# 48 unused matmuls of several tile shapes behind the last output matmul of an attention-plus-SwiGLU kernel

## The chip, the cores and the metric

The kernel runs on one core of one Trainium2 chip. A core has a matrix engine (TensorE, PE in the profile; its weight loads are listed apart as PEld), VectorE (DVE), ScalarE (ACT), GpSimd (POOL) and SyncE (SP), each with its own instruction queue, and 16 DMA engines that the queues feed. The engines meet through semaphores. The metric is the device time of one execution in microseconds, the median over several runs.

TensorE's array has 128 rows (the inputs of a matmul, the contracted dimension) and 128 columns (its outputs). A matmul can be given a part of it, a *tile*: "64x128" is a tile of 64 rows and 128 columns, and its place is named by its first row and column. The stationary operand (the weights) is loaded into the tile, and then the moving operand streams through, one column after another; the result goes to a bank of PSUM. In the profile's rows the tile stands ahead of the shape of the moving operand: `64*128 64x512`.

## The reference

One transformer block with its two branches side by side, for 2048 tokens of width 576, in bf16:

```python
x = A_x
xn = _layernorm(x, axis=-1)
return x + _A_ref(xn, A_wqkv, A_wo) + _B_ref(xn, B_w1, B_w3, B_w2)
```

Branch A is causal attention with 32 heads of 18 and a window of 256 tokens, followed by the projection `wo`; branch B is a gated unit, `silu(xn @ w1) * (xn @ w3)`, 4608 wide, followed by `w2`.

## The kernel before

The kernel writes all instructions into a list by hand, in program order (`_Prog.add`, line 59): each with its engine, the buffers that it reads (`r`), writes anew (`w`) or writes jointly with the ones before (`j`). `resolve` (line 90) works out from these the fewest semaphore waits: a `w` or `j` on a PSUM bank waits for the other engines' reads of what stood there before, while the order within TensorE's own queue needs no semaphore. `replay` (line 130) then issues each engine's list in its own block, and SyncE at its end waits for all output transfers. At the end of the block all engines meet; the instructions of this meeting carry line 1283 in the profile.

The tokens are worked in four chunks of 512. In each chunk TensorE computes the projections to q, k and v, the attention scores (line 621) and the products with v (line 689) in between the 36 units of the gated branch (line 759), and then the second half of the chunk: for both halves of the output's 576 columns, and for four token tiles of 128, it sums `hT @ w2` and `oT @ wo` in one PSUM bank a token tile (`p2_list`, `p2_mm`, line 830). The scores, the units and most of the second half use 64x128 tiles, two at a time, one in each half of the rows. The products with v use 64x20 tiles, eight at a time: two halves of the rows by four groups of columns.

The end of the last chunk is different (`whole` in `p2_list`): the four token tiles are finished one after the other with 128x128 tiles. For token tiles 0 to 2, VectorE adds the residual from the bank to the output buffer `ofin` (line 861) and SyncE sends it (line 863). The last token tile has its sum so far added to the residual ahead of time (`keep`, line 845), and its last part is computed in two cuts of 160 and 128 columns, into two other banks, `ACC[0][0]` and `ACC[0][1]`; each cut is added (line 852) and sent (line 854) by itself. So behind the very last matmul stand one addition over 128 columns, one transfer of 32 KB, SyncE's wait for it, and the meeting of the engines.

The eight PSUM banks in the second half are `ACC[0]` (four banks, first half of the columns) and `ACC[1]` (four banks, second half). `oT` holds the attention's output, transposed, 128 partitions by 5 by 512.

Of the kernel before, what the change touches and what calls it, by code (L numbers as in the profile page):

```python
# [44 lines left out]
class _Prog:  # L45
# [13 lines left out]
    def add(self, eng, fn, r=(), w=(), j=(), dma=None, after=()):  # L59
        deps = []  # L60
        for k in r:
            deps += self.bufs[k].writers
        for k in w:
            g = self.bufs.get(k)
            if g is not None:
                deps += g.ahead(eng)
        for k in j:
            g = self.bufs[k].before
            if g is not None:
                deps += g.ahead(eng)  # L70
        op = _Op(eng, fn, deps + list(after), dma)
        op.after = tuple(after)
        self.n[eng] += 1
        op.pos = self.n[eng]
        if dma is not None:
            self.dma_count[dma] = self.dma_count.get(dma, 0) + 16
            op.cnt = self.dma_count[dma]
        for k in r:
            self.bufs[k].readers.append(op)
        for k in w:  # L80
            self.bufs[k] = _Gen([op], self.bufs.get(k))
        for k in j:
            self.bufs[k].writers.append(op)
        for k in w:
            if self.bufs[k].before is not None:
                self.bufs[k].before.before = None
        self.ops.append(op)
        return op
# [76 lines left out]
def bass_parallel_sum__sliding_block__glu_gated_swiglu__prompt_kernel(  # L165
# [20 lines left out]
    G = H // 4  # L186
# [9 lines left out]
    add = P.add  # L196

    with ExitStack() as es:

        def sb(name, shape, dtype=dt.bfloat16):  # L200
            return es.enter_context(nc.sbuf_tensor(name, shape, dtype))
# [68 lines left out]
        oT = sb("oT", [128, 5, CH])  # L270
# [7 lines left out]
        PS = es.enter_context(nc.psum_tensor("ps", [128, 8, 512], dt.float32))  # L278
        JOBS, SC = ((0, 1), (2, 3), (4, 5)), (6, 7)
        ACC = [[], []]  # L280
# [36 lines left out]
        def load_part(after=(), behind=()):  # L317

            nonlocal nfill
            if nfill >= 6 * NC * NFC:  # L320
                return
            k, i = divmod(nfill, 6)
            s, dst = w13_at(k)
            part, n = divmod(i, 2)
            c0 = (k % NFC) * 512
            src = (B_w3, B_w1)[n]
            nfill += 1
            add("sp", lambda e: e.dma_start(
                dst[64 * n:64 * n + 64, 3 * part:3 * part + 3, :],
                src[192 * part:192 * part + 192, c0:c0 + 512].rearrange("(kd p) f -> p kd f", p=64)),  # L330
                r=list(behind), after=after, dma=f"w13_{s}_{n}", **{"j" if i else "w": [("w13", s)]})
# [5 lines left out]
        def last_pe():  # L337
            return next(o for o in reversed(P.ops) if o.eng == "pe")
# [546 lines left out]
        for t in range(TB):  # L885
# [4 lines left out]
            w=["wv"], dma="wv")  # L890
# [24 lines left out]
        for h in range(2):  # L915
            for n in range(2):
                c0 = n * D + h * HD
# [137 lines left out]
        for c in range(NC):  # L1055
# [13 lines left out]
            start = START[c]  # L1069
# [119 lines left out]
            for u in range(NF):  # L1189
# [46 lines left out]
                if c == 0 and u == 13:  # L1236
                    for t in range(4):
                        r0 = 4 * Dh + 252 * (t // 2)
                        rows = A_wo[r0:r0 + 252, :].rearrange("(s p d) f -> p s d f", p=2, d=Dh)[t % 2, :, :, :]
                        add("sp", lambda e, t=t, rows=rows: e.dma_start(wo[0:126, t, :], rows),  # L1240
                            dma="wo", **{"j" if t else "w": ["wo"]})
                if c == 0 and u == 18:
                    rows = A_wo[0:4 * Dh, :].rearrange("(n d) f -> n d f", d=Dh)
                    add("sp", lambda e: e.dma_start(wo[126:128, 0:4, :], rows[:, 0:2, :].rearrange("n d f -> d n f")),
                        j=["wo"], dma="wo")
                    for p in range(2):
                        add("sp", lambda e, p=p: e.dma_start(wo[64 * p:64 * p + 64, 4, :], rows[:, 2:Dh, :]),
                            j=["wo"], dma="wo")
# [12 lines left out]
            n = -3  # L1261
            for item in p2_list(c):
# [17 lines left out]
                elif n in (170, 195, 220, 245, 270, 295) and c + 1 < NC:  # L1280
                    load_part((last_pe(),))

        with nc.Block() as block:
            P.replay(es, block)

# [27 lines left out]
```

## Time and profile before

| what | value |
|---|---|
| time, median of 3 runs | 554.75 us (554.68 to 554.92) |
| span of the profiled execution, first to last instruction | 553.1 us |
| the page's own time for the profiled execution, beside the span | none given |
| TensorE busy | 549.3 us (99%) |
| mean granted TensorE clock | 1.000 |
| matmuls, weight loads | 8072, 8072 |
| chain of waits, share of TensorE | 98% |

A row of the view in order of time gives start and length in microseconds from the start of the span, engine, line, operation, the names of its output and inputs, the shapes, and the number of instructions that the row merges; in brackets the idle time ahead of it. A group row gives line, engine, operation, names, shapes and count, then busy microseconds and the mean nanoseconds of one. A matmul's length is from its start to the end of its result, so rows of matmuls that follow each other overlap: the pace is read from start to start.

### The profile page before, as it was taken

What the parts mean: (1) busy time and instruction counts of PE and PEld (TensorE: products, weight loads), DVE (VectorE), ACT (ScalarE), POOL (GpSimd) and SP (SyncE); (2) the same over time, 40 slices, a digit from 0 to 9 for tenths busy, and PEclk for the clock granted to TensorE, in tenths of its full rate; (3) what the DMA queues carried; (4) which work ended last, traced back from release to release, by engine and by line L of the source; (5) the groups of instructions that cost most, each with busy time, mean ns of one, the idle gap of its engine ahead of it and who ended that gap; (6) DMA issues with size and microseconds to landing.
All of it is one profiled execution on the core that took longest, in us unless ns stands there. A gap on an engine that the chain in (4) does not pass through costs nothing.

```text
span 553.1 us, 18357 instructions
## 1 busy us (share of the span) xinstructions
PE 549.3 (99%) x8072; PEld 338.3 (61%) x8072; DVE 313.7 (57%) x584; ACT 258.7 (47%) x360; POOL 212.2 (38%) x388
## 2 busy tenths in 40 slices
PE   8999999999999999999999999999999999999998
PEld 6555544777555544577765554558886555455776
DVE  8466797710468886651056988665105567866311
ACT  6456776000288567700047847760005784775000
POOL 6324675400047465530005656643001553663100
PEclk9999999999999999999999999999999999999999
DMA  9998899477577953757746875466773673542750
GB/s 257 211 200 175 190 222 200 129 200 181 141 144 141 181 135 96 181 144 206 185 110 139 175 144 146 117 149 168 191 180 87 138 172 103 150 105 57 194 152 23
DMA packets 128038, 86.00 MB, mean 155 GB/s; under 512 B 35702, under 2 KB 125646, under 8 KB 127958
## 3 DMA queue, kind: packets, MB, share of 16 engines
q1 hardware_dynamic: 89138, 62.80, 49.7%
q10 hardware_dynamic: 38820, 22.02, 15.7%
q8 instruction: 63, 1.03, 0.8%
q14 instruction: 17, 0.14, 0.1%
HBM read 71.29 MB, written 2.36 MB: 133 GB/s over the span
## 4 chain that ended last, share of the span: by engine, by line
PE 98%; DMA 1%; ACT 0%; DVE 0%; issue 0%
PE ps L759 51%; PE ps L830 29%; PE ps L491 10%; PE ps L621 6%; PE ps L689 3%; DMA xp<-in_A_x_dram 1%; DVE stats L394 0%; ACT hT L388 0%; ACT sd L367 0%; PE ps L426 0%; ACT xnT L439 0%; DVE ofin L852 0%; DVE mv L397 0%
## 5 line engine op out<-in xcount | busy, mean ns | idle before, releaser
L759 PE MATMUL ps<-xnT,w 64*128 64x512 bf16 x1400 | 185.3, 376 | 0.0
L759 PE MATMUL ps<-xnS,w 64*128 64x512 bf16 x1120 | 150.6, 376 | 0.0
L830 PE MATMUL ps<-w,hT 64*128 64x288 bf16 x2292 | 143.9, 282 | 0.0
L774 DVE SCALAR_TENSOR_TENSOR gs<-th,ps 128x512 bf16<-128x512 bf16 x144 | 97.9, 680 | 77.8 <-ACT th L768 77.4
L830 PEld LDWEIGHTS ps<-w,hT 64*128 64x128 bf16 x2292 | 115.8, 94 | 26.1 <-issue 0.5
L768 ACT ACTIVATE th<-ps 128x512 bf16<-128x512 f32 x144 | 85.7, 595 | 60.6 <-PE ps L759 59.4
L759 PEld LDWEIGHTS ps<-xnT,w 64*128 64x128 bf16 x1400 | 67.0, 94 | 63.5 <-issue 0.2
L777 DVE SCALAR_TENSOR_TENSOR hT<-gs,ps 128x512 bf16<-128x512 bf16 x144 | 98.9, 687 | 5.0
L658 POOL TENSOR_TENSOR pt<-pt,mk 128x256 bf16<-128x256 bf16 (+1 forms) x143 | 85.6, 623 | 26.3 <-ACT pt L630 26.3
L658 POOL TENSOR_TENSOR hT<-hT,mk 128x256 bf16<-128x256 bf16 (+1 forms) x52 | 30.3, 604 | 161.1 <-ACT hT L630 161.1
L630 ACT ACTIVATE pt<-ps 128x1024 bf16<-128x1024 f32 (+1 forms) x80 | 80.7, 1009 | 24.0 <-PE ps L621 23.3
L759 PEld LDWEIGHTS ps<-xnS,w 64*128 64x128 bf16 x1120 | 53.8, 94 | 50.9
L504 ACT ACTIVATE stage<-ps 128x512 bf16<-128x512 f32 x16 | 9.6, 597 | 139.3 <-PE ps L491 139.3
L861 DVE TENSOR_TENSOR ofin<-ps,xp 128x288 bf16<-128x288 f32 x31 | 12.2, 451 | 98.8 <-PE ps L830 98.8
L621 PE MATMUL ps<-qv,kv 64*128 64x320 bf16 (+4 forms) x528 | 51.5, 260 | 0.0
L621 PEld LDWEIGHTS ps<-qv,kv 64*128 64x128 bf16 x528 | 26.2, 94 | 27.7 <-ACT pt L630 1.0
L491 PE MATMUL ps<-xnT,wp 64*128 64x512 bf16 (+1 forms) x360 | 38.4, 355 | 0.0
L722 DVE STREAM_TRANSPOSE od<-oq 128x256 bf16<-128x256 bf16 x64 | 25.4, 425 | 12.1 <-POOL oq L715 12.1
L630 ACT ACTIVATE hT<-ps 128x1024 bf16<-128x1024 f32 (+1 forms) x28 | 28.4, 1014 | 7.8 <-PE ps L621 7.6
L658 POOL TENSOR_TENSOR stage<-stage,mk 128x256 bf16<-128x256 bf16 (+1 forms) x44 | 24.9, 586 | 14.4 <-ACT stage L630 14.4
L630 ACT ACTIVATE stage<-ps 128x1024 bf16<-128x1024 f32 (+1 forms) x24 | 24.3, 1014 | 7.9 <-PE ps L621 7.8
L491 PEld LDWEIGHTS ps<-xnT,wp 64*128 64x128 bf16 x360 | 18.5, 94 | 14.2
(92 smaller groups left out, 395.1 us busy)
## 6 DMA issues: line engine op xcount, KB each, us to landing
w<-in_B_w_dram SPq DMA_DIRECT2D x210, 192.0 KB, 4.1
w<-in_B_w_dram ACTq DMA_DIRECT2D x70, 288.0 KB, 3.8
xp<-in_A_x_dram SPq DMA_DIRECT2D x29, 144.0 KB, 4.4
out_dram<-ofin SPq DMA_DIRECT2D x31, 72.0 KB, 1.7
xnS<-xnT SPq DMA_DIRECT2D x8, 256.0 KB, 4.6
oT<-od SPq DMA_DIRECT2D x56, 36.0 KB
pt<-in_A_wqkv_dram SPq DMA_DIRECT2D x4, 288.0 KB, 4.9
hT<-in_B_w_dram SPq DMA_DIRECT2D x6, 192.0 KB, 5.9
```

The costliest lines, as they stand in the source:

```text
L491: op = add("pe", lambda e, out_=out_, st=st, mv=mv, n=n, r0=r0, first=first: e.matmul(out_, st, mv, start=first, stop=(part == 1 and n == ...
L621: add("pe", lambda e, r0=r0, out_=out_, kb=kb, q0=q0, nb=nb: e.matmul(out_, kb4[r0:r0 + 64, g, kb + NV - NB, :] if kb < 0 else kv[r0:r0 + ...
L630: add("act", lambda e: e.activation(pt_slot(sl)[:, :, 0:w], PS[:, SC[0]:SC[1] + 1, 0:w], ACT.Exp, scale=scale), r=[("ps", b) for b in SC], ...
L658: add("pool", lambda e, vb=vb, mm=mm: e.tensor_tensor(vb, vb, mm, ALU.mult), r=(key if n == 0 else []) + ["mk"], **{"w" if n == 0 else "j" ...
L689: add("pe", lambda e, p=p, q=q, pr=pr, sl=sl, g=g, pos=pos, q0=q0, nb=nb, col=col, first=first, n=n: e.matmul(PS[32 * q:32 * q + VW, banks ...
L722: add("dve", lambda e: e.transpose(od[i][:, g % 2, c0:c0 + CH // 2], oq[:, c0:c0 + CH // 2]), r=["oq", "oq0"], **{"j" if half or g % 2 els ...
L759: op = add("pe", lambda e, n=n, r0=r0, r=r, k=k, src=src: e.matmul(PS[:, b0 + r, :], wt[r0:r0 + 64, k, fl * 128:(fl + 1) * 128], src, star ...
L768: add("act", lambda e: e.activation(th[i][:], PS[:, bg, :], ACT.Tanh, scale=0.5), r=[("ps", bg)], w=[("th", i)])
L774: add("dve", lambda e: e.scalar_tensor_tensor(out=gs[i][:], in0=th[i][:], scalar=1.0, in1=PS[:, bg, :], op0=ALU.add, op1=ALU.mult), r=[("t ...
L777: add("dve", lambda e: e.scalar_tensor_tensor(out=hT[:, u, :], in0=gs[i][:], scalar=0.5, in1=PS[:, bu, :], op0=ALU.mult, op1=ALU.mult), r= ...
L830: op = add("pe", lambda e: e.matmul(PS[:, bank, 0:w], stat, move, start=new, stop=False, skip_group_check=True, **tile), r=keys, after=hel ...
L861: add("dve", lambda e: e.tensor_tensor(ofin[:, o, :], PS[:, bank, 0:HD], xp[xs[n]][:, d0:d0 + HD], ALU.add), r=[("ps", bank), ("xp", xs[n] ...
```

## The change

Behind the loop over the chunks, thus behind everything in each engine's list, a helper `shape_mm` is defined and called. Each call adds one matmul on TensorE: stationary operand and moving operand are slices of `oT` (its first two 512-column blocks), 256 columns are streamed, and the result goes to one of four banks that nobody reads any more: `ACC[0][2]`, `ACC[0][3]`, `ACC[1][0]`, `ACC[1][1]`. The first call for a bank writes it anew, the later ones jointly.

The first loop takes four shapes (w, h) = (64, 32), (128, 32), (64, 64), (32, 64), two turns of each. A turn is one tile of 64 rows by 128 columns in rows 64 to 127, followed by the tiles of h rows and w columns that fill rows 0 to 63: 4, 2, 2 and 4 of them. The second loop takes two turns of eight tiles of 32 rows and 64 columns that fill the whole array. Together these are 2 x (5 + 3 + 3 + 5) + 2 x 8 = 48 matmuls. (A short description that came with the change speaks of 70.)

```diff
                 elif n in (170, 195, 220, 245, 270, 295) and c + 1 < NC:
                     load_part((last_pe(),))
 
+        free_banks = [ACC[0][2], ACC[0][3], ACC[1][0], ACC[1][1]]
+
+        def shape_mm(b, r0, rows, c0, cols, n, after=()):
+            add("pe", lambda e: e.matmul(
+                PS[c0:c0 + cols, b, 0:n], oT[r0:r0 + rows, 0, 0:cols], oT[r0:r0 + rows, 1, 0:n],
+                start=True, stop=True, tile_position=(r0, c0), skip_group_check=True),
+                r=[("oT", j) for j in range(G // 2)] + ["oTz"], **{"j" if b in opened_banks else "w": [("ps", b)]})
+            opened_banks.add(b)
+
+        opened_banks = set()
+        for w_, h_ in ((64, 32), (128, 32), (64, 64), (32, 64)):
+            for turn in range(2):
+                shape_mm(free_banks[0], 64, 64, 0, 128, 256)
+                for c_ in range(0, 128, w_):
+                    for r_ in range(0, 64, h_):
+                        shape_mm(free_banks[1 + r_ // 32], r_, h_, c_, w_, 256)
+        for turn in range(2):
+            for r_ in range(0, 128, 32):
+                for c_ in range(0, 128, 64):
+                    shape_mm(free_banks[(1, 2, 0, 3)[r_ // 32]], r_, 32, c_, 64, 256)
+
         with nc.Block() as block:
             P.replay(es, block)
```

## The prediction

> **What bounds the kernel now.** I read the engine table of the page first, then the chain of waits, then the last three microseconds in order of time, where the change stands.
>
> ```profile
> span 553.1 us, 18357 instructions
> ...
> PE 549.3 (99%) x8072; PEld 338.3 (61%) x8072; DVE 313.7 (57%) x584; ACT 258.7 (47%) x360; POOL 212.2 (38%) x388
> ...
> PEclk9999999999999999999999999999999999999999
> ...
> 519.90 31.01 PE ps L830 x477
> 550.91 0.02 issue
> 550.94 0.29 DVE ofin L852
> ```
>
> TensorE (PE) is busy for 99% of the span at an ungated clock. The chain of waits ends in an unbroken run of output matmuls of line 830, to 550.91 us, and then one VectorE addition. So anything put in front of that last matmul would cost its full length, and something behind it costs nothing until TensorE finishes later than the rest of the program. What the rest still has to do is this:
>
> ```profile
> 550.46 0.44 PE L830 MATMUL ps<-wo,oT 128*128 128x128 bf16 x5
> ...
> 550.94 0.29 DVE L852 TENSOR_TENSOR ofin<-ps,uq 128x128 bf16<-128x128 f32 x1 [0.18 <-PE ps L830]
> ...
> 551.26 0.34 SPq L854 DMA_DIRECT2D out_dram<-ofin x1
> ...
> out_dram<-ofin SPq DMA_DIRECT2D x1, 32.0 KB, 1.5
> ...
> SPq L1283 <- DMA out_dram<-ofin: 0.4, 1, 0.4
> SPq L1283 <- PEq L1283: 0.2, 1, 0.2
> ...
> 550.91:553.10 2.19, 0.00 (x0) 1.00 0.26 67
> ```
>
> The last five matmuls (first two numbers: start and length of the row) end at 550.46 + 0.44 = 550.90. The addition, the issue of its output transfer at 551.26 and its landing 1.5 us later bring the output home at 551.26 + 1.5 = 552.76. The wait rows of SyncE show the rest: it waits for that transfer, and then all engines meet at the end of the block (line 1283), up to 553.1. In the stretch 550.91 to 553.10 TensorE has no instruction at all: 2.19 us are free under the output transfer. That is the cover of the added matmuls.
>
> **The change part by part.** It removes and moves nothing. Counting its loops: the four pairs (w, h) give 4, 2, 2 and 4 tiles in rows 0 to 63 beside one 64x128 tile in rows 64 to 127, twice each: 2 x (5 + 3 + 3 + 5) = 32 matmuls. The last two turns give 2 x 8 = 16 tiles of 32x64 over all rows. That is 48 matmuls of 256 columns, with 48 weight loads, all on TensorE. (The 70 of the short description I cannot find in the loops; see the rivals.) No transfer, no VectorE, ScalarE or GpSimd instruction is added.
>
> *Waits.* The first write of each of the four banks waits for the VectorE additions that read it. The latest of these is the one of token tile 1 in the last half:
>
> ```profile
> 548.71 0.46 DVE L861 TENSOR_TENSOR ofin<-ps,xp 128x288 bf16<-128x288 f32 x1 [0.64 <-PE ps L830]
> ```
>
> It ends at 549.17, before the first added matmul can start, so these waits cost nothing; without that cover the price would be the 0.46 us of one addition. The last two additions read other banks, and oT was complete before the last `wo` matmuls read it. Nothing stands behind the added matmuls in TensorE's queue except its arrival at the end of the block, and for that every engine waits.
>
> *The pace of one matmul.*
>
> ```profile
> 53.14 1.03 PE L759 MATMUL ps<-xnT,hT 64*128 64x512 bf16 x8
> ...
> L621 PE MATMUL ps<-qv,kv 64*128 64x256 bf16 x48 | 6.6, 269 | 0.0
> ...
> L759 PE MATMUL ps<-xnT,w 64*128 64x512 bf16 x1400 | 185.3, 376 | 0.0
> ```
>
> Eight matmuls of 64x128 tiles, four pairs (one tile in each half of the rows), take 1.03 us, the last alone 0.376: (1.03 - 0.376) / 3 = 0.218 us from pair to pair for 512 columns, 0.424 ns a column. The two halves run side by side, since the pair takes what one would. 256 columns are then 0.108 us of streaming, and the result of a lone one is there 0.27 us after its start (269 ns).
>
> *Small tiles of one shape.*
>
> ```profile
> 52.54 0.31 PE L689 MATMUL ps<-hT,va 64*20 64x320 bf16 x4
> 52.55 0.31 PE L689 MATMUL ps<-pt,va 64*20 64x320 bf16 x4
> 52.68 0.23 PE L689 MATMUL ps<-hT,va 64*20 64x128 bf16 x4
> 52.69 0.23 PE L689 MATMUL ps<-pt,va 64*20 64x128 bf16 x4
> 52.73 0.25 PE L689 MATMUL ps<-hT,va 64*20 64x192 bf16 x4
> 52.74 0.26 PE L689 MATMUL ps<-pt,va 64*20 64x192 bf16 x4
> 52.94 0.37 PE L621 MATMUL ps<-qv,kv 64*128 64x320 bf16 x4
> ```
>
> Eight 64x20 tiles of 320 columns take 0.14 us (52.54 to 52.68), as one alone would (320 x 0.424 = 0.136): tiles of one shape run together, the second four starting 0.01 us behind the first four (52.73 and 52.74), some 3 ns a tile, and their weight loads are hidden. I take this for groups of 32-row tiles too, though no 32-row tile is in this trace.
>
> *A change of shape.* It is dearer:
>
> ```profile
> 51.66 0.40 PE L759 MATMUL ps<-xnT,hT 64*128 64x512 bf16 x2
> 51.99 0.31 PE L689 MATMUL ps<-hT,va 64*20 64x320 bf16 x4
> ...
> 546.08 0.29 PE L830 MATMUL ps<-w,hT 64*128 64x288 bf16 x2
> ...
> 546.29 0.30 PE L830 MATMUL ps<-w,hT 128*128 128x288 bf16 x1
> ...
> 546.43 0.53 PE L830 MATMUL ps<-w,hT 128*128 128x288 bf16 x3
> ```
>
> From 64x128 tiles to 64x20: the second matmul of the pair starts at 51.66 + 0.40 - 0.376 = 51.68 and has streamed its 512 columns at 51.90, but the next shape starts at 51.99: 0.09 us with nothing new. From 64x20 back (fence before): the last of the eight starts at about 52.76 and has streamed 192 columns at 52.84, the next shape starts at 52.94: 0.10. From 64x128 to 128x128: 546.08 + 0.005 + 0.122 = 546.21, next at 546.29: 0.08 to 0.09. Three kinds of change, one price, whichever dimension changes; I take 0.095 us. Behind it the first matmul of the new shape is late by another 0.01 (546.29 to 546.43 is 0.13 to 0.14, where 288 columns take 0.122), since its weights could not be loaded ahead.
>
> In the change, every turn goes 64x128, other shape, 64x128. In all the switches that the trace shows, however, the new tile covers rows of the array that the old one used; there the wait could also be a wait for those very rows. Here the two shapes lie in different halves. The bound from below is thus 0 a switch (they run side by side, as the pairs of one shape do), the bound from above the whole latency of a group with its weight load, 0.27 + 0.09 us. I take 0.095 as in the switches seen: the same price for three kinds of change looks like a property of the whole array, set once for all tiles, rather than of the rows that happen to collide.
>
> Beside these rows the Trainium skill, TensorEngine Tiling (Array Packing), section Tiling Modes, Key Properties, states that a change of tiling mode, as opposed to a change of tile, drains TensorE. By that rule the half in which a tile lies doesn't matter, and the sum would be the one below; the trace agrees as far as each of its switches costs 0.08 to 0.10 us. The same list says that tiles work independently, with loads and matmuls in parallel; if that held between shapes too, the sum would be that of the first rival.
>
> *The sum*, in us of the profiled execution. The last output matmul starts at 550.90 - 0.219 = 550.68 (the row of five ends at 550.90; 219 ns is the mean of that form) and streams 128 columns in 0.055; the first switch of 0.095 follows: 550.83.
>
> ```profile
> L830 PE MATMUL ps<-wo,oT 128*128 128x128 bf16 x5 | 0.4, 219 | 0.0
> ```
>
> Then sixteen groups (eight turns, one 64x128 tile and one group of small ones each), each 0.108 streaming + 0.095 for the switch behind it + 0.01 late weights = 0.213, in all 3.41; sixteen times a further tile of a group starts 3 ns later, 0.05. The last loop begins at 554.29. Its first turn of eight takes 0.108 + 0.01, the second starts at 554.41, its eighth tile at 554.43, and ends at 554.70. That is 3.8 us of added work behind 550.90, under a cover of 2.19. Between the landing of the output (552.76) and the span's end (553.1) lie 0.34 us, of which the meeting of the engines needs a part. How much stands behind the last arrival isn't in the rows: between 0.05 and 0.34, and I take 0.25. The new span is then 554.70 + 0.25 = 554.95, which is 1.85 us above 553.1.
>
> The page gives no time of its own for the profiled execution beside the span; the median of the runs, 554.75, lies 1.65 us above the span, for start and end of the program, which I leave as it is. Forecast: 554.75 + 1.85 = **556.6 us**, 0.33% slower. Its own bounds: no late weights (17 x 0.01 less) and 0.05 instead of 0.25 at the end make it 1.5, so 556.2; if after each switch a whole weight load stands open (94 ns in the row below instead of 10), 17 x 0.084 = 1.4 more, so 558.1.
>
> ```profile
> L830 PEld LDWEIGHTS ps<-w,hT 64*128 64x128 bf16 x2272 | 114.1, 94 | 25.6 <-issue 0.2
> ```
>
> **The rivals.** (1) *Side by side: not slower.* Tiles in different halves don't wait for each other, and only a change of shape in the same rows costs. From 550.83: eight turns of some 0.115, four changes in the lower rows (three between the pairs, one into the last loop) of 0.105, and the last loop's 0.41 end at 552.58. The engines' meeting has to wait for TensorE only from 553.1 - 0.25 = 552.85 on, so it stays hidden with 0.27 us to spare: 554.75, no change. For it speaks that pairs of 64x128 in two halves and eight 64x20 tiles do overlap; against it that the three switches cost the same whichever tiles collide. If the shapes run one after the other but without a switch's cost, sixteen groups of 0.108 end within 0.4 us of the cover, which counts as the same case.
>
> (2) *Half and half.* Only a pair that shares no dimension drains. 32x128 shares the columns and 64x64 the rows of the 64x128 tile; these four turns would then take about 0.115 instead of 0.43 us, 1.25 us less in all: TensorE ends at 553.45, 0.6 us late: 555.35. No row speaks for it: the trace's changes each share a dimension (64x128 to 64x20 the rows, to 128x128 the columns) and still cost 0.09.
>
> (3) *Dearer.* A switch waits for the results, and the load comes after it: a group 0.27 + 0.094 = 0.364 instead of 0.213, 17 x 0.15 = 2.6 more: 559.2. Or 32-row tiles don't run together, 30 matmuls more in sequence at 0.108 = 3.2: 559.8. Against the first stand the three switches, against the second nothing but the waves of 64x20 tiles.
>
> (4) *Other than described.* If 70 matmuls were issued, 22 more at the mean price of (554.70 - 550.83) / 48 = 0.081 us: 1.8 more, 558.4.
>
> **How the numbers follow.** Chances: the forecast 0.65, side by side 0.18, half and half 0.08, dearer 0.07, other than described 0.02. The range goes from the side-by-side case with its scatter (the runs lie at 554.68 to 554.92), 554.5, to the forecast's own upper bound, 558.1; it leaves out the dearer case, the 70, and a little of the forecast's tail. The forecast's own range is 556.2 to 558.1. A measurement of this kernel tells 0.2%, 1.1 us, from no change. Slower by more than that: 0.65 + 0.07 + 0.02 = 0.74. Within it: 0.25, the first two rivals less 0.01, which I leave for faster, for nothing in the change can shorten the chain.
>
> **What would show it.** In the changed kernel's order of time, 64x128 rows of the new line should start about 0.21 us after the small tiles before them and the small ones 0.21 after these; a start within 0.02 us of the 64x128 tile shows rival 1. The two turns of 32x64 should be 0.12 apart. TensorE's last record should end near 554.7, with the last landing of the output still at 552.8; SyncE's wait for TensorE at line 1283 should grow from 0.2 to about 2 us (or stay, if all is hidden). It would be wrong if the switches inside a turn are cheap, if 32-row tiles are slow, or if work ahead of 550.9 us moved.

## The result and the profile after

| | before | after |
|---|---|---|
| time, median (range, runs) | 554.71 us (554.50 to 554.92, 6) | 557.12 us (556.53 to 559.57, 6) |
| ratio, 95% interval | | 1.0049 (1.0030 to 1.0067) |
| span of the profiled execution | 553.1 us | 557.8 us |
| end of the last output matmul to end of span | 2.2 us | 4.1 us |

The change costs 2.4 us in the median, 1.7 to 3.7 by the interval. The page's first lines and the end of the chain of waits of the changed kernel:

```profile
span 557.8 us, 18452 instructions
...
PE 554.6 (99%) x8119; PEld 334.7 (60%) x8120; DVE 313.9 (56%) x584; ACT 259.1 (46%) x360; POOL 212.7 (38%) x388
...
513.65 40.06 PE ps L830 x625
553.71 3.83 PE ps L1286 x48
```

The chain no longer ends in the output's addition and transfer, but in 48 matmuls of the new line 1286, 3.83 us long. Its last stretch in order of time (start, length, engine, line), the wait rows of SyncE, and the groups by shape:

```profile
553.27 0.44 PE L830 MATMUL ps<-wo,oT 128*128 128x128 bf16 x5
...
553.65 0.28 PE L1286 MATMUL ps<-oT 64*128 64x256 bf16 x1
...
553.86 0.30 PE L1286 MATMUL ps<-oT 32*64 32x256 bf16 x4
...
554.09 0.28 PE L1286 MATMUL ps<-oT 64*128 64x256 bf16 x1
...
554.30 0.30 PE L1286 MATMUL ps<-oT 32*64 32x256 bf16 x4
...
553.65 3.90 PE L1286 MATMUL ps<-oT 64*128 64x256 bf16 x48
...
SPq L1304 <- PEq L1304: 2.1, 1, 2.1
...
out_dram<-ofin SPq DMA_DIRECT2D x1, 32.0 KB, 1.5
...
L1286 PE MATMUL ps<-oT 64*128 64x256 bf16 x8 | 2.2, 280 | 0.0
L1286 PE MATMUL ps<-oT 32*64 32x256 bf16 x24 | 1.0, 284 | 0.0
```

The first 64x128 tile starts at 553.65. The four 32x64 tiles, in the other half of the rows and free to run beside it, start 0.21 us later; the next 64x128 tile starts 0.23 us after these. Had the two halves run together, 553.86 would read 553.65. The last result is there at 553.65 + 3.90 = 557.55, the span ends at 557.8. The output still lands 1.5 us after its issue, and SyncE, which waited 0.2 us for TensorE at the end of the block (now line 1304), waits 2.1.

This profiled execution is the slowest of its six, and only 1.9 us of its 4.7 us over the span of before lie in that stretch. The rest was lost at its start, before the code that the change adds:

```profile
PE ps L491 <- DMA wv<-in_A_wqkv_dram: 1.9, 1, 1.9
...
5.00:9.00 4.00, 1.85 (x42) 1.00 1.10 315
9.00:12.50 3.50, 3.50 (x44) 0.52 0.85 223
12.50:20.00 7.50, 7.50 (x96) 1.00 1.02 232
```

A load of weights from memory came late, TensorE waited 1.9 us for it, and in the next 3.5 us the clock (the share behind the instruction count) was granted at 0.52.

### The profile page after: what moved, and what is told of

Read it like the earlier page. It is cut to its first block, busy times and chain, and to the rows that moved or that the text cites. A ratio compares the mean times of both kernels' runs of the same rounds, so it can differ in the third digit from the quotient of the medians.

```text
span 557.8 us, 18452 instructions
## 1 busy us (share of the span) xinstructions
PE 554.6 (99%) x8119; PEld 334.7 (60%) x8120; DVE 313.9 (56%) x584; ACT 259.1 (46%) x360; POOL 212.7 (38%) x388
## 4 chain that ended last, share of the span: by engine, by line
PE 98%; DMA 1%; SPq 0%; issue 0%
PE ps L759 50%; PE ps L830 29%; PE ps L491 10%; PE ps L621 6%; PE ps L689 3%; DMA wv<-in_A_wqkv_dram 1%; PE ps L1286 1%; PE ps L426 0%; SPq L304 0%
## 5 line engine op out<-in xcount | busy, mean ns | idle before, releaser
L830 PEld LDWEIGHTS ps<-w,hT 64*128 64x128 bf16 x2292 | 112.2, 94 | 29.6 <-issue 0.2
```

Source lines behind the costliest of these rows:

```text
L830: op = add("pe", lambda e: e.matmul(PS[:, bank, 0:w], stat, move, start=new, stop=False, skip_group_check=True, **tile), r=keys, after=hel ...
```

## The experiments

The theory: every change of tile shape drains the whole array, wherever the tiles lie, at a fixed price of about 0.1 us; 17 changes carry TensorE past the end of the output. Rivals: the tiles have a price of their own; the price follows the length of the matmuls; and, for the scatter of the runs, the longer code, the start, or the clock. "Stretch" is the time from the end of the last output matmul to the end of the span. The kernel before ran beside each group: 554.82 us with the first four, 554.85 with the second four, 554.75 with the last two. (One of e5's eleven runs took 3322 us, which nothing here explains; it is left out of the range and the ratio, and the median moves by less than 0.1 us with or without it.)

| run | edit to the added part | time, us | ratio, 95% interval | stretch, us |
|---|---|---|---|---|
| e1 | none | 557.14 (556.52 to 558.15) | 1.0026 to 1.0052 | 4.1 |
| e2 | one shape, 48 matmuls | 556.37 (554.83 to 557.72) | 1.0011 to 1.0039 | 4.2 |
| e3 | the change's 48, sorted by shape | 555.22 (555.03 to 555.66) | 0.9996 to 1.0015 | 2.8 |
| e4 | 64 columns instead of 256 | 555.13 (555.00 to 555.73) | 0.9997 to 1.0015 | 2.7 |
| e5 | one shape, 40 matmuls | 554.81 (554.53 to 555.48) | 0.9989 to 1.0007 | 2.2 |
| e6 | the change less its last 8 | 556.64 (556.23 to 557.36) | 1.0020 to 1.0045 | 4.3 |
| e7 | eight turns a shape instead of two | 571.93 (571.80 to 572.80) | 1.0296 to 1.0324 | 19.7 |
| e8 | halves by columns, 22 matmuls | 555.46 (555.28 to 555.99) | 1.0003 to 1.0022 | 2.9 |
| e9 | e7's matmuls, sorted by shape | 560.90 (560.57 to 561.35) | 1.0094 to 1.0127 | 8.1 |
| e10 | e7 with 512 columns | 585.68 (584.65 to 586.22) | 1.0536 to 1.0568 | 33.5 |

### e1: the change again

> The changed kernel once more, unaltered. Theory (every change of tile shape drains the whole array): the stretch from the end of the last output matmul to the span's end is again 4.1 us (2.2 in the kernel before). If the late start of its first profile (a load awaited for 1.9 us and a halved clock for 3.4 us, together about 2.8 us) was a chance of single executions, some runs lie at 554.75 + 1.85 = 556.6 and the others up to 3 us above, and the first 10 us of the trace look like those of the kernel before or not, as it falls. If the added code itself shifts the start, all runs lie above 556.6.

This time the profile caught the fastest run (556.52), with nothing lost at the start. First the kernel before at its start (window and its length, busy time and count of TensorE, granted clock, DMA share, GB/s), then e1 (busy time and count of PE, PEld, DVE, ACT and POOL in place of TensorE's alone):

```profile
5.00:10.00 5.00, 4.23 (x88) 1.00 1.12 317
10.00:15.00 5.00, 5.00 (x70) 1.00 1.14 245
```

```profile
5.00:10.00 5.00, 4.69 (x91) 3.09 (x91) 4.53 (x16) 3.81 (x12) 1.00 (x4) 1.00 1.12 301
10.00:15.00 5.00, 5.00 (x70) 3.10 (x68) 3.79 (x9) 3.26 (x8) 4.79 (x18) 1.00 1.15 253
550.66:554.80 4.14, 3.84 (x49) 1.65 (x48) 0.29 (x1) 0.00 (x0) 0.00 (x0) 1.00 0.15 40
```

The stretch is the same 4.1 us (550.66 to 554.8) at full clock. So it belongs to the change, and the late start of the first profile to that execution. Three of the change's eleven runs lie at 556.52 to 556.57, which is 1.7 to 1.9 us above the medians of before; the others scatter above.

### e3 and e4: order and length

```diff
-        for w_, h_ in ((64, 32), (128, 32), (64, 64), (32, 64)):
+        for turn in range(8):
+            shape_mm(free_banks[0], 64, 64, 0, 128, 256)
+        for w_, h_ in ((128, 32), (64, 64), (32, 64), (64, 32)):
             for turn in range(2):
-                shape_mm(free_banks[0], 64, 64, 0, 128, 256)
```

> The same 48 matmuls as in the change, sorted by shape: all eight 64x128 first, then 32x128, 64x64, 64x32, 32x64. Theory: five changes of shape instead of seventeen, twelve times 0.105 = 1.3 us less: +0.5 us, 555.3, stretch behind the last output matmul 2.7 us. Rival (price by matmul, not by order): +1.85, stretch 4.1.

In e4 each of the three calls has 64 columns:

```diff
-                shape_mm(free_banks[0], 64, 64, 0, 128, 256)
+                shape_mm(free_banks[0], 64, 64, 0, 128, 64)
...
-                        shape_mm(free_banks[1 + r_ // 32], r_, h_, c_, w_, 256)
+                        shape_mm(free_banks[1 + r_ // 32], r_, h_, c_, w_, 64)
...
-                    shape_mm(free_banks[(1, 2, 0, 3)[r_ // 32]], r_, 32, c_, 64, 256)
+                    shape_mm(free_banks[(1, 2, 0, 3)[r_ // 32]], r_, 32, c_, 64, 64)
```

> The change with 64 columns a matmul instead of 256. Theory (a drain of fixed length behind the streaming): sixteen groups of 0.027 + 0.105 instead of 0.108 + 0.105: about 1.4 us less, +0.4 us, 555.2, stretch behind the last output matmul 2.6 us; the start of one group lies 0.13 us behind the start of the one before. Rival (the switch's price follows the length of the matmul ahead of it): a quarter of 0.215, thus 0.05 from group to group, hidden, 554.7, stretch 2.2.

Last output matmuls and first added ones, e3 and then e4:

```profile
550.22 0.44 PE L830 MATMUL ps<-wo,oT 128*128 128x128 bf16 x5
550.60 2.59 PE L1286 MATMUL ps<-oT 64*128 64x256 bf16 x48
```

```profile
550.64 0.44 PE L830 MATMUL ps<-wo,oT 128*128 128x128 bf16 x5
...
551.02 0.20 PE L1286 MATMUL ps<-oT 64*128 64x64 bf16 x1
...
551.15 0.35 PE L1286 MATMUL ps<-oT 32*64 32x64 bf16 x5
```

The same 48 matmuls in another order take 2.59 us instead of 3.90: 1.31 less for twelve changes fewer, 0.11 a change. It is the order, not the tiles. And with 64 columns the next shape starts 0.13 us after the one before (551.02 to 551.15), of which 64 x 0.424 ns = 0.03 is streaming: 0.10 a change, as with 256 columns. The price doesn't follow the length. The times alone tell neither run from no change (both intervals include it); the stretches of 2.8 and 2.7 us, against 2.2 and 4.1, are clear.

### e2 and e5: one shape, and a block of instructions

```diff
-        for w_, h_ in ((64, 32), (128, 32), (64, 64), (32, 64)):
...
-        for turn in range(2):
+        for turn in range(6):
             for r_ in range(0, 128, 32):
                 for c_ in range(0, 128, 64):
```

> The same number of added matmuls, 48 of 256 columns, but all in the one shape 32x64, six turns of eight over the whole array. Theory: one change of shape only, so 0.105 + 6 x 0.11 + 0.3 us; TensorE ends 0.95 us behind the last output matmul's start plus 0.15, under the output transfer; 0.0 us, 554.7, stretch behind the last output matmul 2.2 us. Rival (each small matmul has a price of its own, 1.85 us / 48): +1.8 us, stretch 4.1. If the late start comes with the added code's size, it comes here too, since the code is as long.

The measured 556.37 and 4.2 us are the rival's numbers. The trace says otherwise. TensorE and the waits of SyncE in e2:

```profile
551.72 0.86 PE L1286 MATMUL ps<-oT 32*64 32x256 bf16 x48
...
SPq L1298 <- DMA out_dram<-ofin: 2.3, 1, 2.3
...
SPq L1298 <- PEq L1298: 0.2, 1, 0.2
...
out_dram<-ofin SPq DMA_DIRECT2D x1, 32.0 KB, 3.4
...
q8 instruction: 64, 1.05, 0.8%
```

The 48 matmuls are over in 0.86 us, at 552.58; nobody waits for them. SyncE waits 2.3 us for the last output transfer instead of 0.4, since it lands 3.4 us after its issue instead of 1.5. The page shows 64 instruction transfers; before it were 63. In the packet records the 64th, 16 KB, is on its way from 553.04 to 554.45. Of the 128 packets of the last output, 120 start between 552.99 and 553.24, and the last eight, one DMA engine's share, only from 554.44 on. That they stood behind the block on one engine is inferred: the records don't name engines. The profiled run is the slowest of the six. Of the 2.8 us by which its span is longer than that of before (555.97 - 553.14), 1.9 are in the stretch; 0.9 was lost earlier, since its last output matmul ends at 551.79 instead of 550.90. Two of the six spans, 553.1 and 553.2, are no longer than before, so the same code doesn't lose this time in every run. e5 tests the block, against e2:

```diff
-        for turn in range(6):
+        for turn in range(5):
             for r_ in range(0, 128, 32):
```

> One shape as in the second experiment, but five turns (40 matmuls) instead of six. Theory on the 1.6 us lost there: the 86th added TensorE instruction (the 43rd matmul) makes the instruction queue fetch a 64th block of 16 KB, 1.5 us behind the last output matmul, and the last output packets stand behind that block on their DMA engine. With 80 instructions the block isn't fetched: 63 blocks, last output lands 1.5 us after its issue, 554.8, stretch behind the last output matmul 2.2 us. Rival (matmuls of 32x64 tiles or their PSUM writes hold up the output): five sixths of the loss, about 556.2.

```profile
550.77 0.75 PE L1286 MATMUL ps<-oT 32*64 32x256 bf16 x40
...
SPq L1298 <- DMA out_dram<-ofin: 0.4, 1, 0.4
...
out_dram<-ofin SPq DMA_DIRECT2D x1, 32.0 KB, 1.5
...
q8 instruction: 63, 1.03, 0.8%
```

With 16 instructions fewer there is no 64th block, the output lands after 1.5 us, and 40 added matmuls cost nothing that can be measured. The loss in e2's stretch goes with the block. The change has a 64th block too, but its matmuls come more slowly. In e1 the last output is issued at 551.02 and lands 1.5 us later, and from 552.70 to the end of the span one packet is left, the block's, which starts at 553.96 and delays nothing:

```profile
DMA packets 1, 0.02 MB, mean 8 GB/s; under 512 B 0, under 2 KB 0, under 8 KB 0
...
q8 instruction: 1, 0.02, 2.8%
```

### e8: halves by columns

```diff
-        for w_, h_ in ((64, 32), (128, 32), (64, 64), (32, 64)):
+        for w_, h_ in ((64, 64), (32, 128), (32, 64)):
             for turn in range(2):
-                shape_mm(free_banks[0], 64, 64, 0, 128, 256)
-                for c_ in range(0, 128, w_):
-                    for r_ in range(0, 64, h_):
-                        shape_mm(free_banks[1 + r_ // 32], r_, h_, c_, w_, 256)
-        for turn in range(2):
...
+                shape_mm(free_banks[0], 0, 128, 0, 64, 256)
+                for c_ in range(64, 128, w_):
+                    for r_ in range(0, 128, h_):
+                        shape_mm(free_banks[1 + r_ // h_], r_, h_, c_, w_, 256)
```

> The halves turned: a 128x64 tile in columns 0 to 63 next to 64x64, 128x32 and 64x32 tiles in columns 64 to 127, two turns each, 22 matmuls in twelve groups. Theory (a change of shape drains the whole array): 0.1 + 11 x 0.215 + 0.3 from 550.73, stretch behind the last output matmul 2.9 us, +0.65 us, 555.4. Rival (tiles in different columns don't wait for each other, though those in different rows do): hidden, 554.75, stretch 2.2 us.

```profile
550.95 0.30 PE L1286 MATMUL ps<-oT 128*64 128x256 bf16 x1
...
551.18 0.52 PE L1286 MATMUL ps<-oT 64*64 64x256 bf16 x3
```

The 64x64 tiles in the other columns start 0.23 us after the 128x64 tile. The stretch of 2.9 us and 555.46 are the theory's numbers: it makes no difference whether the tiles are apart by rows or by columns. But in the change the neighbours lie in different rows and in the same columns, and here in different columns and in the same rows. Tiles in opposite corners, which share neither, were not tried.

### e6, e7, e9 and e10: the clock

e6, 40 matmuls, against the change:

```diff
-        for turn in range(2):
+        for turn in range(1):
             for r_ in range(0, 128, 32):
```

> The change less the last turn of its second loop: 40 matmuls. Theory (drains): 0.12 us less than the change, 556.45 in its undisturbed runs, stretch 4.0 us; no 64th block of instructions. If the scatter of the change's runs (556.5 to 559.6) comes with that block, all runs here lie within 0.3 us; if it comes from the clock, which was granted to 0.999 in the slower runs and 1.000 in the fastest, they scatter up to 557.5 as before.

e7, against the change:

```diff
         for w_, h_ in ((64, 32), (128, 32), (64, 64), (32, 64)):
-            for turn in range(2):
+            for turn in range(8):
```

> Eight turns of each pair of shapes instead of two: 48 groups more at the 0.217 us from group to group that the change's trace shows. Theory (fixed price, full clock): 10.4 us more than the change, 567.0, stretch behind the last output matmul 14.5 us, clock 1.00 throughout. Rival (the array is so little used between drains that the clock is withdrawn, which would also be the scatter of the change's runs): the granted clock falls to 0.5 in that stretch, groups of 0.3 us or more, 570 or more.

The last output matmuls, the added ones and windows of TensorE in e6, the slowest of its runs, then windows in e7 (time busy, instructions, granted clock, DMA share, GB/s) and two starts in e7:

```profile
550.58 0.44 PE L830 MATMUL ps<-wo,oT 128*128 128x128 bf16 x5
550.96 4.12 PE L1286 MATMUL ps<-oT 64*128 64x256 bf16 x40
...
550.80:552.80 2.00, 2.00 (x22) 1.00 0.28 74
552.80:554.07 1.27, 1.27 (x12) 1.00 0.00 0
554.07:555.30 1.23, 1.01 (x14) 0.50 0.00 0
```

```profile
553.00:555.00 2.00, 2.00 (x23) 0.98 0.03 8
555.00:557.00 2.00, 2.00 (x12) 0.50 0.00 0
...
569.00:570.10 1.10, 0.80 (x20) 0.50 0.00 0
...
555.27 0.39 PE L1286 MATMUL ps<-oT 64*128 64x256 bf16 x1
...
555.59 0.71 PE L1286 MATMUL ps<-oT 32*128 32x256 bf16 x3
```

In e6 there is no 64th block, and the runs scatter all the same: 556.23, 556.27 and 556.64 at a mean clock of 1.000, 557.08 and 557.36 at 0.998 and 0.999. In the profiled one, TensorE is still at work when its clock is halved at 554.07. That explains only a part: the added matmuls end 555.08 - 551.02 = 4.06 us behind the last output matmul, where the change less one turn would give 3.84 - 0.12 = 3.72, so the halved clock cost 0.3 us of the 1.1 by which this run lies above the fastest. In e7 the same happens at about 554.9, and the clock doesn't come back to the end, 15 us later, though TensorE counts as busy throughout; a change of shape with its group then takes 0.32 us (555.27 to 555.59) instead of 0.217. My theory of a full clock fell, 571.93 instead of 567.0; the rival stands. But is it the gaps, or that only half of the array works? e9 sorts e7's matmuls; against e3:

```diff
-        for turn in range(8):
+        for turn in range(32):
             shape_mm(free_banks[0], 64, 64, 0, 128, 256)
         for w_, h_ in ((128, 32), (64, 64), (32, 64), (64, 32)):
-            for turn in range(2):
+            for turn in range(8):
```

> The matmuls of the seventh experiment sorted by shape: 32 of 64x128, then eight turns each of the other four shapes, then the last loop; five changes of shape, and never more than half of the array's rows at work until the last loop. Theory (the clock is withdrawn because the drains leave the array without a stream for half of the time): the clock stays at 1.00, stretch behind the last output matmul 8.1 us, 560.6. Rival (it is withdrawn because only half of the array works): the clock falls to 0.5 some 3.4 to 6.8 us into the stretch, 562 or more.

e10 is e7 with `512` for each `256`, as e4 had `64`:

> The seventh experiment with 512 columns a matmul, so that a group streams 0.216 us in each 0.325 (two thirds) instead of 0.108 in 0.217 (half). Theory (share of time with a stream decides, and the threshold lies between): the clock stays at 1.00, stretch behind the last output matmul 22 us, 574.4. Rival (any such share withdraws it): clock 0.5 after one to two windows of 3.4 us, groups of 0.5 us, 585 or more.

First e9, then e10:

```profile
553.00:555.00 2.00, 2.00 (x27) 1.00 0.03 8
555.00:557.00 2.00, 2.00 (x52) 1.00 0.00 0
557.00:558.80 1.80, 1.54 (x60) 1.00 0.00 0
```

```profile
553.00:555.00 2.00, 2.00 (x19) 0.86 0.03 8
555.00:557.00 2.00, 2.00 (x11) 0.50 0.00 0
...
580.00:584.00 4.00, 3.77 (x31) 0.50 0.00 0
```

In e9 only half of the rows work for 6 us, but with five changes of shape in all, and the clock stays: 560.90 where 560.6 was expected. So half an array alone doesn't withdraw it. In e10 the array streams for two thirds of the time and the clock goes all the same; that the limit lay between half and two thirds was wrong. With half of the rows at work it takes the gaps. Whether gaps would also do it with the whole array at work between them wasn't tried: the share of the array and of the time together, a quarter in e7 and a third in e10, where the clock went, and a half in e9, where it stayed, would divide the runs as well.

## Why the prediction was right

*The cover.* 2.19 us free behind the last output matmul: e5's 40 matmuls fit under it at no cost, and the change's landing after 1.5 us shows the output itself untouched.

*The price of a change of shape,* 0.095 + 0.01 us, taken from three switches whose tiles overlap and carried over to tiles that don't: 0.10 in e4, 0.11 in e3, and 0.10 to 0.12 in the change (0.21 to 0.23 from group to group, less 0.11 of streaming). The choice of "a property of the whole array" was the step on which all hung, and it held for tiles apart by rows (the change) and by columns (e8). TensorE's work behind the last output matmul ends 557.55 - 553.71 = 3.84 us after that matmul; 554.70 - 550.90 = 3.80 was forecast. Here the Trainium skill's rule (TensorEngine Tiling (Array Packing), section Tiling Modes, Key Properties: a change of mode drains TensorE) is borne out also for tiles that share no rows with their neighbours, with 0.21 to 0.23 us from group to group in the change, and for tiles that share no columns, with 0.23 in e8; the independence that the same list grants to tiles shows in these runs within one shape only.

*Small tiles of 32 rows* run together: e5's 40 take 0.75 us, 0.27 to 0.29 of it the last result.

*The end,* taken as 0.25 us behind TensorE's last result: 557.83 - 557.55 = 0.28. In sum the stretch grew by 4.1 - 2.2 = 1.9 us; 1.85 was forecast.

*The rivals.* Side by side, and half and half, fell with the starts of the change's trace. The dearer case fell with the same starts and e5. The 70 matmuls fell with the count of 48.

*Slips in the working,* none of which moves the forecast. "Half and half" counts four turns whose pair shares a dimension, but the 64x32 tiles also share their 64 rows with the 64x128 tile. So six of the eight turns would have been cheap, TensorE would have ended at 554.70 - 6 x 0.31 = 552.8, and that rival gives no change in time instead of 555.35. In "dearer", the 30 matmuls in sequence count the 64-row tiles too; for 32-row tiles alone they are 22, 2.4 us. The upper bound adds up to 558.0.

*What was missed.* First, the sentence that no transfer is added: 96 more instructions (48 matmuls and 48 weight loads, of which the page records 95) come with a 64th block of 16 KB. It cost nothing in the two profiled executions of the change, by the luck of its moment; in e2 the output landed 1.9 us later with it, and the median rose by 1.6. Second, what lies beyond the stretch. The forecast of 556.6 is the time of the change's fastest runs (556.52 to 556.57), while the median lies 0.5 us higher. The comparison flatters it a little: it sets the fastest runs of the change against a median of before, whose own fastest are 554.50 and 554.58, and fastest against fastest the change costs 1.9 to 2.0 us. The sum took the clock as full, and e6 shows, for a kernel eight matmuls shorter, that it can be halved while the added matmuls run. But that cost 0.3 us there and can't be the whole of it: a mean clock of 1.000, to three places, leaves room for less than 0.0005 x 556 = 0.28 us of lost clock, and two slower runs of the change with that mean have spans of 555.4 and 555.8, 0.6 and 1.0 above the 554.8 of the fastest. The kernel before scatters too, from 554.58 to 555.99 beside e1. None of the change's slower runs was profiled but the one with its loss at the start, so the cause of the 0.5 us stays open. The range's upper end was drawn for weight loads, not for this, and that it held the median was luck.

## What to carry to other kernels

Matmuls of different tile shapes didn't run side by side here, neither in different rows nor in different columns: each change costs about 0.1 us that no other tile fills, so sort matmuls by shape. Where only half of the array works between them, many such gaps in a row cost twice, because the clock is withdrawn and what follows is slower (e7, e10). And instructions appended to an engine that has ended can cost more than their run time (e2): look at the number of instruction transfers and at where the last one falls.

## What the hardware showed beyond expectation

TensorE at 100% busy lost half of its clock: in e7 and e10 the profile's busy time is full in the windows from 555 us on, at 0.50 granted. Busy counts a matmul to the end of its result, so it hides the gaps of some 0.1 us (at full clock) in which nothing new streams. The Trainium skill describes short idle times between groups of matmuls that make the clock swing (TensorE: Matmul & The Clock Gate, section on a second failure mode of the clock gate); these runs agree as far as short gaps are enough, but here the clock didn't swing: it stayed at 0.50 for 15 us in e7 and about 30 us in e10.

One instruction block of 16 KB, 1.4 us on its way, came with a landing of a 32 KB output after 3.4 us instead of 1.5 (e2), though the DMA engines were otherwise nearly idle; without the block (e5) it was 1.5 again.
